# A linear-attention and expert-routing kernel: a new order of the first batch, four scaled-q buffers, loads and DMA transposes in strict turns, and the second expert's weight sums moved up into block 7

## The chip, the cores and the metric

The kernel runs on one core of a Trainium2 chip. The metric is device time in microseconds (us) of a whole execution, compared by medians and by ratios of the same rounds. The engines are called PE (TensorE), DVE (VectorE), ACT (ScalarE), POOL (GpSimd, which issues the loads) and SP (SyncE, which issues the DMA transposes).

## The reference, cut to what matters

```python
def _attn_ref(q, k, v):                      # (8, 8, 576, 64) each
    # phi(x) = concat(relu(x) * cos, relu(x) * sin) over the head dimension
    q_p, k_p = phi(q, cos_w, sin_w), phi(k, cos_w, sin_w)
    kv = np.einsum('bhsf,bhsd->bhfd', k_p, v)
    z = np.sum(k_p, axis=2)
    num = np.einsum('bhsf,bhfd->bhsd', q_p, kv)
    den = np.einsum('bhsf,bhf->bhs', q_p, z)[..., None] + 1e-06
    return num / den

def _moe_ref(x, w_gate, w1, w2):             # x (4608, 512), 8 experts, F = 1024
    P = np.exp(logits - logits.max())        # logits = x @ w_gate
    for _ in range(8):                       # the normalisation
        P /= P.sum(1, keepdims=True) + 1e-09
        P /= P.sum(0, keepdims=True) + 1e-09
        P *= N / E
    for e in range(E):
        out += P[:, e:e+1] * (np.maximum(x @ w1[e], 0.0) @ w2[e])
```

## The kernel before

The first stage is a pipeline of blocks. In block j, PE does the first expert's feed-forward for 512 tokens (16 "slots": eight of first-layer products, eight of w2 products). Between the slots stands the attention of the next batch, and the preparation of the one after it. For each batch there are two kinds of transfer: loads of q, k and v (six of 288 KB, issued by POOL), and, from the third batch on, four DMA transposes of the scaled q (issued by SP). PE reads the transposed q (in the views q_pT, acc_lo and acc_hi by the buffer that holds it) for the denominators of the next block. From block 7 on, the normalisation of the routing runs beside the products: DVE adds up P over the tokens of each partition (colp), and PE adds colp over the partitions (the product copied_ps<-colp). Stage 2, with the second expert, follows.

```python
qp_pool = p1.enter_context(tc.tile_pool(name="qp_pool", bufs=3))   # scaled q
...
def load(b, half, names="qkv", held_back=False):
    for name in names:
        ...
        i = nc.gpsimd.dma_start(out=..., in_=view[:, 2 * half : 2 * half + 2])
        if held_back:
            after(ve.last, i)            # wait for the last DVE instruction written so far
        landing[name, b, half] = i

def prep_q(b, hk):
    ...
    q_p = qp_pool.tile([P, C, 2, D], F16, name="q_p")
    ve.tensor_tensor(out=q_p[:], in0=q16..., in1=cs, op=ALU.mult)
    if by_dma:                           # b >= 2
        turned = nc.sync.dma_start(out=qTs[b, hk], in_=q_p[:]..., transpose=True)
        if b == 3 and hk == 0:
            after(landing["v", b, 1], turned)
...
# which work stands behind which slot of block j (b = j + 1); cut
for slot, fn, hk in (
    (4, prep_q, 0), (5, prep_q, 1), (8, prep_k, 0), (8, prep_q, 2),
    (9, prep_k, 1), (10, prep_kv, 0), (10, prep_k, 2), (12, prep_q, 3),
    (12, prep_kv, 1), (12, prep_k, 3), (13, prep_kv, 2), (14, prep_kp, 3),
    (14, prep_v, 3),
) if j == 1 else (
    (4, prep_q, 0), (5, prep_k, 0), (5, prep_q, 1), (6, prep_k, 1), ...
) if j == 2 else (
    (3, prep_k, 0), (4, prep_k, 1), (5, prep_q, 0), (6, prep_q, 1), ...
):
    at(j, slot, fn, b + 1, hk)
if j == 1:
    at(j, 15, sums, b + 1, 0)
    for name in "qkv":
        for half in range(2):
            at(j, 12, load, b + 2, half, name, True)
elif j and b + 2 < B:
    for half in range(2):
        at(j, 11 + half, load, b + 2, half, "qkv", True)
```

So with batches counted from one, block 1 holds the fourth batch's preparation and issues the fifth's loads; block 2 holds the fifth's preparation and issues the sixth's loads; block 3 holds the sixth's preparation, whose first k (a relu on ACT) stands in slot 3.

The second expert uses a seven-product scheme that needs sums of its w2. Before the change, DVE makes them when the second expert's first pair of row tiles begins:

```python
if name == "P1":
    if self.first:
        ve.tensor_tensor(out=tw2[0], in0=b22, in1=b12, op=ALU.subtract)
        ve.tensor_tensor(out=tw2[1], in0=tw2[0], in1=b11, op=ALU.subtract)
...
elif name == "P7":
    if self.first:
        ve.tensor_tensor(out=tw2[2], in0=b21, in1=tw2[0], op=ALU.subtract)
```

Of the kernel before, what the change touches and what calls it, by code (L numbers as in the profile page):

```python
# [25 lines left out]
def kernel(  # L26
# [185 lines left out]
    with ExitStack() as p1:  # L212
        ld = p1.enter_context(tc.tile_pool(name="ld", bufs=4))
        kp_pool = p1.enter_context(tc.tile_pool(name="kp_pool", bufs=4))
        qp_pool = p1.enter_context(tc.tile_pool(name="qp_pool", bufs=3))
        qT_pool = p1.enter_context(tc.tile_pool(name="qT_pool", bufs=1))
        kv_pool = p1.enter_context(tc.tile_pool(name="kv_pool", bufs=2))
        rb_pool = p1.enter_context(tc.tile_pool(name="rb_pool", bufs=4))
# [7 lines left out]
        landing = {}  # L226
        sources = {"q": q, "k": k, "v": v}

        def load(b, half, names="qkv", held_back=False):
            for name in names:  # L230
                x = ld.tile([P, 2, C, D], F16, name=f"{name}_ld")
                view = sources[name][b].rearrange("(hk hh) (p c) d -> (hh p) hk (c d)", hh=2, c=C)
                i = nc.gpsimd.dma_start(  # L233
                    out=x[:].rearrange("p hk c d -> p hk (c d)"),
                    in_=view[:, 2 * half : 2 * half + 2],
                )
                if held_back:

                    after(ve.last, i)
                landing[name, b, half] = i  # L240
                for i in range(2):
                    loaded[name, b, 2 * half + i] = x[:, i]
# [5 lines left out]
        load(0, 0, "q")  # L248
        gidx = cs_pool.tile([P, C], FP32, name="gidx")
# [4 lines left out]

        ones_sq = cs_pool.tile([P, P], F16, name="ones_sq")
# [6 lines left out]
        load(0, 1, "q")  # L262
        for name in "kv":
            load(0, 0, name)
            load(0, 1, name)
# [22 lines left out]
        for _ in range(74):  # L288
            keep_busy(1)
# [17 lines left out]
        for hh in range(2):  # L307
            ve.tensor_copy(
                out=cs_half[hh * HP : (hh + 1) * HP, :, :, hh],
                in_=cs[hh * HP : (hh + 1) * HP, :, :, 0],  # L310
            )
# [8 lines left out]
        C3 = C // 3  # L320

# [6 lines left out]
        with nc.allow_low_precision("sums of zeros and ones"):  # L328
# [11 lines left out]
        ones_col = const.tile([P, 1], FP32, name="ones_col")  # L340
        ve.memset(ones_col[:], 1.0)
        ones_all = const.tile([P, P], FP32, name="ones_all")
        ve.memset(ones_all[:], 1.0)
        eps_row = cs_pool.tile([1, 32], FP32, name="eps_row")
        ve.memset(eps_row[:], 1e-6 / XS)
# [8 lines left out]
        lent = acc_lo[:, G_LO - 4 : G_LO, :].rearrange("p g d -> p (g d)").bitcast(F16)  # L354
        VA = C * (D + 2)
        v_augs = [
            lent[:, i * VA : (i + 1) * VA].rearrange("p (c d) -> p c d", d=D + 2)
            for i in range(4)
        ]
# [7 lines left out]
        for t in v_augs:  # L367
            ve.memset(t[:, :, D : D + 1], 1.0 / XS)

# [7 lines left out]
        def prep_q(b, hk):  # L377

            q16 = loaded.pop(("q", b, hk))
            by_dma = b >= 2  # L380
            if by_dma:
                ve.tensor_scalar(
                    out=q16, in0=q16, scalar1=0.0, scalar2=None, op0=ALU.max
                )
            q_p = qp_pool.tile([P, C, 2, D], F16, name="q_p")
            ve.tensor_tensor(
                out=q_p[:], in0=q16.unsqueeze(2).to_broadcast([P, C, 2, D]),
                in1=cs, op=ALU.mult,
            )
            if by_dma:  # L390
                qTs[b, hk] = q_pTs[(b * HK + hk) % len(q_pTs)]
                turned = nc.sync.dma_start(
                    out=qTs[b, hk], in_=q_p[:].rearrange("p c a d -> p (c a d)"),
                    transpose=True,
                )
                if b == 3 and hk == 0:

                    after(landing["v", b, 1], turned)
            else:
                qps[b, hk] = q_p  # L400
# [76 lines left out]
        def sums_begun(b, half):  # L477
# [7 lines left out]
            kv_ps = [ps_s.tile([P, 512], FP32, name="small_ps") for hh in range(2)]  # L485
# [157 lines left out]
        for hk in range(HK):  # L643
            if hk == 3:
                prep_k(0, 0)
                prep_k(0, 1)
                z_ps = key_sums(0)
                prep_q(0, hk)
                key_sums_made(0, z_ps)
            else:  # L650
                prep_q(0, hk)
            for i in range(3):
                turn(0, hk, i, True)
                keep_busy(3)
        prep_kp(0, 0)
        prep_kp(0, 1)
        denominators(0, range(0, 4))
        keep_busy(8)
        for hk in (2, 3):
            prep_k(0, hk)  # L660
        z_ps = key_sums(1)
        prep_kp(0, 2)
        key_sums_made(1, z_ps)
        prep_kp(0, 3)
        keep_busy(5)
        denominators(0, range(4, 8))
        for half in range(2):
            sums_made(0, half, sums_begun(0, half))
            keep_busy((0, 18)[half])
# [6 lines left out]
        ]  # L676
        for hk in range(HK):
            attend(0, hk)
            for kt in ((), (0,), (1,), (2, 3))[hk]:
                for ft, h_ps in enumerate(first_ps):  # L680
                    te.matmul(
                        out=h_ps[:],
                        lhsT=w0[0][:, kt, ft * P : (ft + 1) * P],
                        rhs=xT[:, kt, 0:TCH],
                        start=(kt == 0),
                        stop=(kt == KT - 1),
                    )
                    if kt == KT - 1:
                        se.activation(out=hT[:, ft, 0:TCH], in_=h_ps[:], func=AF.Relu)
            for i in ((), (0,), (1, 2), ())[hk]:  # L690
                prep_k(1, i, i < 2)
            for i in ((), (0,), (1,), (2, 3))[hk]:
                if i == 3:
                    prep_k(1, i, False)
                prep_kp(1, i)
# [3 lines left out]
        for j in range(B):  # L699
            b = j + 1  # L700
            if j == 0:
# [4 lines left out]
                for hk in range(HK):  # L706
                    for i in range(3):
                        at(0, (5, 6, 6, 7)[hk], turn, 1, hk, i, i != 1)
                    if hk == 0:
                        at(0, 5, prep_q, 1, 3)  # L710
                    if hk == 2:
                        at(0, 6, prep_v, 1, 0, se.copy)
                        at(0, 6, prep_v, 1, 2, ve.tensor_copy)
                    if hk == 3:
                        at(0, 7, prep_v, 1, 1, se.copy)
                        at(0, 7, prep_v, 1, 3, ve.tensor_copy)
# [6 lines left out]
            elif b < B:  # L723
# [14 lines left out]
                elif j == 2:  # L738
                    at(j, 0, sums, b, 1)
                else:  # L740
                    at(j, 0, prep_kv, b, 2)
                    at(j, 1, prep_kv, b, 3)
                    at(j, 2, sums, b, 0)
                    at(j, 2, sums, b, 1)
                at(j, 6 if j == 1 else 3 if j == 2 else 4, denominators, b)
# [18 lines left out]
            elif b + 1 < B:  # L764
                for slot, fn, hk in (
                    (4, prep_q, 0), (5, prep_q, 1), (8, prep_k, 0), (8, prep_q, 2),
                    (9, prep_k, 1), (10, prep_kv, 0), (10, prep_k, 2), (12, prep_q, 3),
                    (12, prep_kv, 1), (12, prep_k, 3), (13, prep_kv, 2), (14, prep_kp, 3),
                    (14, prep_v, 3),
                ) if j == 1 else (  # L770
                    (4, prep_q, 0), (5, prep_k, 0), (5, prep_q, 1), (6, prep_k, 1),
                    (8, prep_q, 2), (8, prep_k, 2), (10, prep_q, 3), (10, prep_k, 3),
# [7 lines left out]
                if j == 1:  # L780
                    at(j, 15, sums, b + 1, 0)
            if j == 1:
                for name in "qkv":
                    for half in range(2):
                        at(j, 12, load, b + 2, half, name, True)
            elif j and b + 2 < B:
                for half in range(2):
                    at(j, 11 + half, load, b + 2, half, "qkv", True)
# [164 lines left out]
    class Pair:  # L953
# [45 lines left out]
        def step(self, name):  # L999
# [3 lines left out]
            if name == "P1":  # L1003
                if self.first:

                    tw2[0:2] = [t_pool.tile([P, FH, DH], F16, name=f"V{k_}")[:] for k_ in (2, 3)]
                    ve.tensor_tensor(out=tw2[0], in0=b22, in1=b12, op=ALU.subtract)
                    ve.tensor_tensor(out=tw2[1], in0=tw2[0], in1=b11, op=ALU.subtract)
# [4 lines left out]
            elif name == "P7":  # L1013

                if self.first:
                    tw2[2:3] = [t_pool.tile([P, FH, DH], F16, name="V4")[:]]
                    ve.tensor_tensor(out=tw2[2], in0=b21, in1=tw2[0], op=ALU.subtract)
# [36 lines left out]
    tw2 = [None] * 3  # L1054
    both = (nc.sync, nc.scalar)
# [92 lines left out]
    for j in range(B - 1, NJ):  # L1148
# [5 lines left out]
        for slot in range(NS):  # L1154
# [6 lines left out]
            if j == B - 1 and slot == 0:  # L1161
                gates(B - 1, Z[:])
            balanced({1: 3, 4: 5, 8: 5, 13: 5, 17: 5, 22: 5}.get((j - B + 1) * NS + slot, 0))
# [24 lines left out]
    def start_fill():  # L1188

        nonlocal k_fill  # L1190
        for _ in range(1 + (k_fill % 14 == 1)):
# [18 lines left out]
    for e in range(1, E):  # L1210
# [3 lines left out]
        for n in range(NU):  # L1214
# [28 lines left out]
            if e == 1 and n == 0:  # L1243
# [4 lines left out]
                w2_first(w)  # L1248
# [45 lines left out]
```

## Time and profile before

| | before |
|---|---|
| median | 975.19 us of 3 runs (974.3 to 975.83) |
| profiled span | 972.1 us, mean granted clock 0.999 |
| PE busy | 959.4 us (99%) |
| DVE / ACT / POOL busy | 807.4 / 565.0 / 60.7 us |

PE is nearly always busy, so only what makes PE wait, or what removes a wait of PE, can show in the time. The prediction below shows the lines.

### The profile page before, as it was taken

To read this page: it belongs to the slowest core of one execution; us is meant where nothing else is said; L and a number is where in the kernel's file an instruction comes from. 1 tells how busy PE (TensorE), PEld (TensorE's weight loads), DVE (VectorE), ACT (ScalarE), POOL (GpSimd) and SP (SyncE) were. 2 spreads that over 40 slices of the span, in tenths; PEclk is the share of its full clock that TensorE was granted. 3 is DMA by queue.
4 is the path that set the end of the run, shared out by engine and by line. 5 is a ranking of instruction groups with operands and counts; after the bars stand their busy time and mean duration, and the time that the engine had idled before them with its cause. 6 is when DMAs were issued, how large, how long until landed. Compare 5 with 4: busy or idle time off the path is not lost.

```text
span 972.1 us, 20258 instructions
## 1 busy us (share of the span) xinstructions
PE 959.4 (99%) x7855; PEld 674.6 (69%) x7855; DVE 807.4 (83%) x1831; ACT 565.0 (58%) x1264; POOL 60.7 (6%) x82
## 2 busy tenths in 40 slices
PE   9999999999999999999999999999999999999997
PEld 6545555567777777777777777777777777777775
DVE  7767776789898887987888987987888987987887
ACT  5767665577776555555555555555555555555551
POOL 6231210010000000000000000000000000000001
PEclk9999999999999999999999999999999999999999
DMA  9999988231004301332004301322004401115435
GB/s 162 188 154 173 156 137 184 44 69 50 26 26 93 69 25 50 68 62 57 25 26 93 69 25 51 68 54 65 26 25 86 75 25 42 33 28 124 123 90 127
DMA packets 81200, 74.72 MB, mean 77 GB/s; under 512 B 33360, under 2 KB 73040, under 8 KB 81104
## 3 DMA queue, kind: packets, MB, share of 16 engines
q0 software_dynamic: 27232, 30.94, 20.4%
q1 hardware_dynamic: 53632, 42.24, 17.8%
q8 instruction: 61, 1.00, 0.4%
q14 instruction: 35, 0.29, 0.1%
q10 hardware_dynamic: 240, 0.26, 0.1%
HBM read 84.30 MB, written 12.98 MB: 100 GB/s over the span
## 4 chain that ended last, share of the span: by engine, by line
PE 91%; DMA 4%; issue 2%; DVE 1%; POOL 1%; ACT 0%; POOLq 0%; DVEq 0%; SPq 0%; ACTq 0%
PE rows_ps L109 34%; PE h_ps L109 28%; PE p_ps L109 11%; PE copied_ps L109 11%; PE y_ps L109 4%; PE small_ps L109 3%; DMA k_ld<-in_k_dram 1%; DMA w1e<-in_moe_w_dram 1%; DMA w2e<-in_moe_w_dram 1%; DVE acc_hi L975 0%; POOL q_ld L233 0%; POOL hs_last L990 0%; DMA out_dram<-acc_lo 0%; DVE H L905 0%; DVE S L203 0%
## 5 line engine op out<-in xcount | busy, mean ns | idle before, releaser
L975 DVE SCALAR_TENSOR_TENSOR acc_lo<-rows_ps,P_tok,acc_lo 128x512 f32<-128x512 f32 (+1 forms) x322 | 203.8, 642 | 74.9 <-PE rows_ps L109 74.8
L109 PEld LDWEIGHTS <-H 128*128 128x128 f16 x2080 | 203.1, 98 | 82.3 <-issue 1.4
L911 ACT CAST u<-h_ps 128x384 f16<-128x384 f32 x288 | 137.5, 478 | 129.7 <-PE h_ps L109 129.7
L109 PEld LDWEIGHTS <-w1e 128*128 128x128 f16 x1632 | 157.7, 98 | 67.2 <-issue 5.3
L905 DVE CUSTOM_DVE_ANT_0 H<-p_ps,u 128x384 f16<-128x384 f32 x329 | 181.7, 552 | 7.2 <-PE p_ps L109 7.1
L109 PEld LDWEIGHTS <-hs 128*128 128x128 f16 x1500 | 146.6, 98 | 56.2
L109 PE MATMUL p_ps<-xT,T 128*128 128x384 f16 x672 | 164.2, 326 | 1.0 <-DVE H L905 0.9
L109 PE MATMUL h_ps<-S,w1e 128*128 128x384 f16 x672 | 164.2, 326 | 0.8 <-ACT u L911 0.6
L109 PE MATMUL rows_ps<-V,H 128*128 128x256 f16 x1000 | 150.0, 273 | 0.7 <-DVE acc_hi L975 0.7
L109 PE MATMUL rows_ps<-w2e,hs 128*128 128x256 f16 x1000 | 150.0, 273 | 0.0
L109 PE MATMUL h_ps<-xT,w1e 128*128 128x384 f16 (+1 forms) x616 | 148.8, 351 | 0.1
L943 ACT ACTIVATE H<-h_ps 128x384 f16<-128x384 f32 x144 | 70.6, 490 | 94.5 <-PE h_ps L109 94.5
L109 PEld LDWEIGHTS <-T 128*128 128x128 f16 x1008 | 98.4, 98 | 31.9 <-issue 4.9
L109 PE MATMUL rows_ps<-w2e,H 128*128 128x256 f16 (+1 forms) x568 | 94.4, 285 | 0.0
L924 ACT COPY copied_ps<-h_ps 128x384 f32<-128x384 f32 x144 | 67.5, 469 | 36.0 <-PE h_ps L109 35.2
L934 ACT ACTIVATE H<-copied_ps 128x384 f16<-128x384 f32 x144 | 70.8, 492 | 20.4 <-PE copied_ps L109 20.4
L109 PE MATMUL h_ps<-S,T 128*128 128x384 f16 x336 | 81.8, 325 | 0.6 <-ACT copied_ps L109 0.5
L109 PE MATMUL copied_ps<-xT,w1e 128*128 128x384 f16 x336 | 82.1, 326 | 0.0
L109 PE MATMUL copied_ps<-w2e,H 128*128 128x256 f16 x504 | 75.6, 273 | 0.0
L109 PE MATMUL rows_ps<-V,hs 128*128 128x256 f16 x500 | 75.0, 273 | 0.0
L975 DVE SCALAR_TENSOR_TENSOR acc_lo<-copied_ps,P_tok,acc_lo 128x256 f32<-128x256 f32 x126 | 60.3, 479 | 0.4
L975 DVE SCALAR_TENSOR_TENSOR acc_hi<-rows_ps,P_tok,acc_hi 128x512 f32<-128x512 f32 (+1 forms) x56 | 41.4, 739 | 20.6 <-PE rows_ps L109 19.7
(146 smaller groups left out, 947.7 us busy)
## 6 DMA issues: line engine op xcount, KB each, us to landing
S<-x_saved SPq DMA_DIRECT2D x114, 192.0 KB, 2.4
out_dram<-acc_lo SPq DMA_DIRECT2D x62, 128.0 KB, 2.4
w1e<-in_moe_w_dram POOLq DMA_DIRECT2D x7, 1024.0 KB, 8.8
w2e<-in_moe_w_dram POOLq DMA_DIRECT2D x7, 1024.0 KB, 9.6
q_ld<-in_q_dram POOLq DMA_DIRECT2D x16, 288.0 KB, 6.5
k_ld<-in_k_dram POOLq DMA_DIRECT2D x16, 288.0 KB, 7.8
v_ld<-in_v_dram POOLq DMA_DIRECT2D x16, 288.0 KB, 9.6
x_saved<-S SPq DMA_DIRECT2D x12, 192.0 KB, 1.8
```

The costliest lines, as they stand in the source:

```text
L109: i = getattr(self.engine, name)(*args, **kwargs)
L905: latest = ve._custom_dve(TENSOR_ADD_SAT, out=out, in0=ps[:, 0:TU], in1=t[:], s0=FP32_MAX, s1=0.0)
L911: se.copy(out=t[:], in_=ps[:, 0:TU])
L924: se.copy(out=Y[:, 0:TU], in_=X[:, 0:TU])
L934: se.activation(out=h11, in_=Y[:, 0:TU], func=AF.Relu)
L943: se.activation(out=h12, in_=X[:, 0:TU], func=AF.Relu)
L975: ve.scalar_tensor_tensor(out=a, in0=rows, scalar=P_tok[:, g, self.e : self.e + 1], in1=a, op0=ALU.mult, op1=ALU.add,)
```

## The change

The intent is to get the first expert products going earlier, to take small waits out of the second and third blocks, to keep loads and transposes from running into one another, and to move the w2 sums out of a stretch in which DVE is full. The diff, cut to its core:

```diff
-        qp_pool = ...(name="qp_pool", bufs=3)
+        qp_pool = ...(name="qp_pool", bufs=4)
-        rb_pool = ...(name="rb_pool", bufs=4)
+        rb_pool = ...(name="rb_pool", bufs=3)
+        turnings = {}
...
-                if held_back:
+                if behind is not None:
+                    after(turnings[behind], i)       # a load waits for a landed transpose
+                elif held_back:
                     after(ve.last, i)
...
-                if b == 3 and hk == 0:
+                if b in (3, 4):                      # a transpose waits for the batch's last v
                     after(landing["v", b, 1], turned)
+                turnings[b, hk] = turned
...     # the first batch: loads, scalings, sums and first products in a new order
-        for _ in range(74):
-            keep_busy(1)                             # 128 columns each
+        for _ in range(110):
+            te.matmul(...)                           # 64 columns each
...     # the slots of the fourth and the fifth batch
-                    (4, prep_q, 0), (5, prep_q, 1), (8, prep_k, 0), (8, prep_q, 2),
-                    (9, prep_k, 1), (10, prep_kv, 0), (10, prep_k, 2), (12, prep_q, 3),
-                    (12, prep_kv, 1), (12, prep_k, 3), (13, prep_kv, 2), (14, prep_kp, 3),
-                    (14, prep_v, 3),
+                    (4, prep_q, 0), (5, prep_q, 1), (9, prep_k, 0), (8, prep_q, 2),
+                    (10, prep_k, 1), (12, prep_q, 3), (12, prep_k, 2), (13, prep_k, 3),
+                    (13, prep_kv, 0), (14, prep_kv, 1),
                 ) if j == 1 else (
-                    (4, prep_q, 0), (5, prep_k, 0), (5, prep_q, 1), (6, prep_k, 1),
-                    (8, prep_q, 2), (8, prep_k, 2), (10, prep_q, 3), (10, prep_k, 3),
+                    (5, prep_q, 0), (6, prep_q, 1), (8, prep_k, 0), (8, prep_q, 2),
+                    (9, prep_k, 1), (10, prep_q, 3), (10, prep_k, 2), (11, prep_k, 3),
...
-                        at(j, 12, load, b + 2, half, name, True)
+                        at(j, 12, load, b + 2, half, name, True, (b + 1, HK - 1))
...
-                    at(j, 11 + half, load, b + 2, half, "qkv", True)
+                    at(j, 11 + half, load, b + 2, half, "qkv", True,
+                       (b + 1, HK - 1) if j == 2 else None)
...     # the second expert's w2 sums, in block 7
             if j == B - 1 and slot == 0:
                 gates(B - 1, Z[:])
+                w2_first(w_next)
+                w2_sums(w_next[1], 0)
+            if j == B - 1 and slot == 2:
+                w2_sums(w_next[1], 1)
```

## The prediction

> **What bounds the kernel now.** I read the page's busy line first, then busy time by stretches, the timelines of the engines at the places that the change touches, the waits, and the landing times of the DMAs.
>
> ```profile
> PE 959.4 (99%) x7855; PEld 674.6 (69%) x7855; DVE 807.4 (83%) x1831; ACT 565.0 (58%) x1264; POOL 60.7 (6%) x82
> ```
>
> TensorE (PE) is busy in all but 12.7 of 972.1 us, so moving work of other engines pays only where PE waits, and a new wait of PE costs its full length. The 12.7 us are the start (1.1), the end, and a few holes. Behind "busy" hides one more thing: filler products on a tile of ones. The first 74 take 5.7 us, and from 7 to 20 us another 4.4 us of PE is filler (summed from the timeline).
>
> The timelines, in order of time, one engine a row:
>
> ```profile
> 1.14 5.72 PE L109 MATMUL y_ps<-ones_sq 128*128 128x128 f16 x74 [1.14 <-DVE ones_sq L109]
> ...
> 6.83 0.77 DVE L109 TENSOR_TENSOR q_p<-q_ld,acc_hi 128x1152 f16<-128x1152 f16 x1
> ...
> 10.50 0.53 DVE L109 TENSOR_SCALAR k_ld<-k_ld 128x576 f16<-128x576 f16 x2 [1.57 <-DMA k_ld<-in_k_dram]
> ...
> 15.50 1.35 DVE L109 RECIPROCAL den<-y_ps 96x192 f32<-96x192 f32 x1
> ...
> 33.78 1.04 PE L109 MATMUL y_ps<-w2e,hT 128*128 128x512 f16 x4
> ...
> 57.89 0.68 ACT L109 ACTIVATE k_ld<-k_ld 128x576 f16<-128x576 f16 x1 [2.25 <-DMA k_ld<-in_k_dram]
> ...
> 59.48 0.46 PE L109 MATMUL small_ps<-hl,acc_hi 96*128 96x192 f16 x3 [1.11 <-ACT rb L109]
> ...
> 84.10 0.72 POOL L233 DMA_DIRECT2D q_ld<-in_q_dram  x1 [13.47 <-DVE acc_lo L109]
> ...
> 91.16 0.68 ACT L109 ACTIVATE k_ld<-k_ld 128x576 f16<-128x576 f16 x1
> ...
> 93.58 1.89 PE L109 MATMUL h_ps<-xT,w1e 128*128 128x512 f16 x8
> ...
> 163.39 0.45 DVE L109 TENSOR_REDUCE rs<-P_tok 128x36 f32<-128x288 f32 x1 [2.20 <-ACT P_tok L109]
> ...
> 166.34 0.28 PE L109 MATMUL copied_ps<-colp,ones_all 128*128 128x8 f32 x2
> ...
> 205.62 0.48 PE L109 MATMUL p_ps<-xT,T 128*128 128x384 f16 x2 [0.85 <-DVE H L905]
> ```
>
> The reader is to see: the first chain (q scaled at 6.83, k at 10.50 when it lands, reciprocal at 15.50) that decides when real products begin; a PE hole of 1.11 us at 59.48 because ACT sat on a k that had not landed; k of the sixth batch used at 91.16 without a wait, close behind its landing at 90.27; the normalisation that begins at 163.39 and feeds PE at 166.34; a hole at 205.62 behind DVE.
>
> By stretches (PE first), the last place:
>
> ```profile
> 200.00:210.00 10.00, 9.01 (x62) 5.86 (x61) 9.93 (x22) 6.69 (x15) 2.59 (x3) 1.00 0.85 157
> ```
>
> DVE is full (9.93) and PE idle for 1.0 us. The landing of w2 of the second expert, from the DMA view of its issue:
>
> ```profile
> w2e<-in_moe_w_dram POOLq DMA_DIRECT2D x1, 1024.0 KB, 17.4
> ```
>
> It is issued at 147.90, so it lands at 165.3.
>
> **What the skill says.** "TensorE: Matmul & The Clock Gate", Part 1: products of the first ~3.4 us run at half clock, and an idle window of the same length throttles again. The 74 products average 5.72/74 = 77 ns against 54 later, so it agrees; the filler must warm, and holes of 1 to 2 us should not cool. The same page's table calls the ACT and DVE queues strict FIFO; 57.89 to 59.48 shows it (a late k holds copies that were ready). "DMA: Bandwidth & Descriptors", "Issuing engines are not separate DMA queues": loads and transposes share 16 engines. Here a transpose issued at 53.6 among loads took 10.2 us to land, others 3.2 to 3.3. Same page, "Anatomy of one DMA", gives about 2.0 us plus bytes/436e9, an estimate of 2.7 us for 288 KB; the trace has 4.7 us for the first load of a group and 1.45 us for each next. I use the trace.
>
> **Part by part.** Sums are of trace durations; "before clock" means the old trace's time.
>
> *First batch.* Three copies and memsets move out of the way, so DVE reaches the first q at about 5.9 instead of 6.83; q lands at 5.95, so 5.97. Four scalings of 0.70 and the halved cosine copy (0.5) end at 9.3. k still lands at 10.47 (the load queue is full from 3 to 41 us, so order alone doesn't hasten it). From there: relu 0.5, k sums on PE to 11.7, DVE to 12.0, relu 0.5, scaled k 0.7, second k sums to 13.3, DVE 13.6, scaled k 14.3, then reciprocal 14.3 against 15.50: 1.2 us earlier. The numerators and first expert products follow with fewer holes, about 1.4 us ahead at the end of the first four column blocks (23.6 against 25.0). Then DVE binds: four scaled k (0.7), two relus (0.25), four scaled q (0.7), four evictions of turns (0.5) and now all four v copies (0.37) run from 22.6 to 32.2; the last sums need 0.65, so w2 products begin at 32.9 against 33.78. **-0.9 us.** w2 pieces land at 30.5 to 34.3, so they just hold.
>
> *Fourth batch.* k goes from slot 8 to 9, behind the copies that PE needs. Its landing, 57.87 before, comes about 1.5 us earlier, as no transpose runs among those loads. The hole of 1.11 and crumbs go: **-1.2 us.**
>
> *Strict turns.* The chain is loads(4th), transposes(4th), loads(5th), transposes(5th), loads(6th). Loads(4th) are issued at 51.03-0.9 = 50.1; five land by 50.1+4.75+4x1.45 = 60.7, say 60.9. Transposes: issued 1.4 apart, landing 3.3 after issue: last at 60.9+4.2+3.3 = 68.4. Loads(5th): six, 68.5+4.75+5x1.45 = 80.5. Transposes(5th): 88.0. Loads(6th): issued 88.1 instead of 84.10; q 92.9, k 94.3 (before 90.27). The slots of the fifth batch were moved back to fit; those of the sixth were not: ACT takes its k in slot 3, on the new clock at 91.16-2.1 = 89.1. ACT blocks until 94.3, PE has two banks and stops at its slot 6, due at 93.58-2.1 = 91.5, until 94.3+0.57+0.55 = 95.4. **+3.9 us**, and k's second half at 98.7 another +0.2.
>
> *w2 sums in block 7.* DVE gets the first difference and two sums after slot 0 of block 7. They read w2, which lands at 165.3, and DVE is in order. So 0.65+0.6+0.6 follow 165.3 and the normalisation starts at 167.15, not 163.39; its first column sums (1.15 to start, 0.67 long and 0.2 margin) are ready at 169.2, and PE, due at 166.34, waits 2.9, then 0.3 at the second. **+3.2 us.** The hole at 200 to 210 goes: idle 1.0 and looser spacing, **-1.2 us.**
>
> *Four q buffers, three reciprocal buffers:* DVE waits once, 1.2 us at 82.0, for a q buffer, off PE's path. **0.**
>
> Sum: -0.9-1.2+3.9+0.2+3.2-1.2 = **+4.0**, that is 979.2 us.
>
> **Rivals.** (a) *The turns are the gain.* Loads and transposes alone run faster than mixed, so k of the sixth batch may come in time. For: 10.2 against 3.3 us. Against: adding up even the fast durations gives 94.3. It would make 979.2-4.1 = 975. (b) *w2 lands earlier or the normalisation has slack.* For: the load shares engines with stores of sums. Against: nothing in the change moves its issue. It would make 979.2-3.2 = 976; with (a), 972. (c) *The opening gains more*, if DVE isn't the binder up to 32 us: up to 2 us more, but w2's last piece at 34.3 caps it. (d) The stop of 3.9 us cools PE (an idle window of about 3.4 us): 1 to 2 us more, 981.
>
> **Range and chances.** Both added waits come from adding landings, not from a view of the new kernel, and such slots were surely placed by someone who looked; I give each about 0.65. 979.2 less about a third of 7.3 is 976.8; I say **977.0 us**. Both waits absent and a better opening is 971, everything and a cooled clock 982: range **971 to 982**. 2% is 19.5 us; nothing here reaches that: faster 0.01, same 0.98, slower 0.01.
>
> **What would show it.** Reciprocal near 14.3; first w2 products near 32.9; no PE hole near 58; ACT idle some 5 us before a k_ld relu near 94 and PE idle some 4 us just behind; DVE idle in block 7 until w2 lands, then PE idle about 3 us ahead of the first product of colp; no hole near 205. If those two PE holes are missing, the time is 971 to 973 and my steps on landings are wrong. If the opening is wrong, DVE's work from 22 to 32 us will show idle time.

## The result, and the profile after

| | before | after |
|---|---|---|
| median, same chip | 975.51 us of 4 runs (974.3 to 979.88) | 986.47 us of 4 runs (985.04 to 987.24) |
| profiled span, mean granted clock | 972.1 us, 0.999 | 985.5 us, 0.994 |

The ratio is 1.0102, 95% interval 1.0069 to 1.0136: slower, by less than 2%. A ratio here is the mean time of one kernel's runs over the mean of the other's of the same rounds, so it is not quite the ratio of the medians. The prediction of 977.0 us, and its range of 971 to 982, missed.

The page of after has PE 2.5 us busier and the span 13.4 us longer:

```profile
PE 961.9 (98%) x7886; PEld 674.6 (68%) x7886; DVE 809.4 (82%) x1834; ACT 564.2 (57%) x1261; POOL 60.4 (6%) x82
```

To see where the time went, I took the start of the same PE instruction in both traces (us from the start of the span; the "predicted" column adds up the prediction's own steps):

```
first w2 product of block     before     after    difference   predicted
0                              33.78     32.25      -1.53        -0.9
1                              54.84     53.24      -1.60        -0.9
2                              76.47     73.78      -2.69        -2.1
3                              95.55    105.47      +9.92        +1.8
4                             114.48    125.39     +10.91        +2.0
6                             152.43    163.26     +10.83        +2.0
first product of colp         166.34    180.11     +13.77        +4.9
first product of stage 2      184.69    198.80     +14.11        +5.2
29th such product             247.79    260.50     +12.71        +4.0
last product                  967.80    980.67     +12.87        +4.0
```

Down to block 2 the rows move about as predicted (the opening gains 0.6 us more than said); then one step fails: from block 2 to block 3 the kernel loses 12.6 us instead of 3.9, and another 1.0 (predicted 0.2) up to block 4. The waits of PE in the stretch from 15 to 215 us of after (who waited, on what: us in total, times, longest) name it:

```profile
PE h_ps L109 <- ACT hT L109: 7.1, 1, 7.1
PE copied_ps L109 <- DVE colp L109: 2.8, 1, 2.8
PE small_ps L109 <- DMA q_pT<-q_p: 1.8, 1, 1.8
PE small_ps L109 <- DVE xT L109: 1.3, 1, 1.3
PE small_ps L109 <- DMA acc_hi<-q_p: 0.5, 1, 0.5
```

The timelines of after at the places the prediction named (start us, us, engine, what, then in brackets the idle time before it and what ended that):

```profile
13.82 1.35 DVE L109 RECIPROCAL den<-y_ps 96x192 f32<-96x192 f32 x1
...
32.25 1.04 PE L109 MATMUL y_ps<-w2e,hT 128*128 128x512 f16 x4
...
92.76 0.35 PE L109 MATMUL small_ps<-q_pT,zsel 128*32 128x192 f16 x6 [1.78 <-DMA q_pT<-q_p]
...
93.28 0.72 POOL L234 DMA_DIRECT2D q_ld<-in_q_dram  x1 [18.24 <-DMA q_pT<-q_p]
...
100.40 0.68 ACT L109 ACTIVATE k_ld<-k_ld 128x576 f16<-128x576 f16 x1 [10.25 <-DMA k_ld<-in_k_dram]
...
101.62 3.57 PE L109 MATMUL h_ps<-xT,w1e 128*128 128x512 f16 x8 [7.06 <-ACT hT L109]
...
175.94 0.69 DVE L109 TENSOR_TENSOR w2e<-w2e 128x1024 f16<-128x1024 f16 x1 [3.92 <-DMA w2e<-in_moe_w_dram]
...
178.01 0.45 DVE L109 TENSOR_REDUCE rs<-P_tok 128x36 f32<-128x288 f32 x1
...
180.11 0.39 PE L109 MATMUL copied_ps<-colp,ones_all 128*128 128x8 f32 x2 [2.78 <-DVE colp L109]
```

The reader is to see the predicted chain in the predicted order, only later: the sixth batch's loads go out at 93.28, when the last transpose of the fifth has landed; ACT sits 10.25 us on the first k, which lands at 100.38; PE stands 7.06 us behind ACT. The stop also cools PE's clock: the eight products at 101.62 take 3.57 us, where the same group took 1.89 in before (93.58). By stretches (after the engines' busy times come the granted clock of PE, the DMA share and GB/s):

```profile
96.00:98.00 2.00, 0.00 (x0) 0.00 (x0) 0.51 (x2) 0.00 (x0) 1.59 (x3) 0.83 1.19 192
98.00:100.00 2.00, 0.00 (x0) 0.00 (x0) 1.54 (x3) 0.00 (x0) 0.00 (x0) 0.50 1.02 127
...
106.00:108.00 2.00, 2.00 (x9) 0.94 (x8) 0.00 (x0) 1.27 (x4) 0.00 (x0) 0.61 1.30 136
```

The clock records put half clock from 97.31 to 107.55 us.

The chain that the prediction added up, against the trace of after (landing times):

```
step                                 predicted    after    added lateness
loads of the fourth batch, last v       60.9      60.72        -0.2
transposes of the fourth, last          68.4      70.20        +2.0
loads of the fifth, last v              80.5      83.54        +1.2
transposes of the fifth, last           88.0      92.72        +1.7
loads of the sixth, first k             94.3     100.38        +1.4
PE goes on in block 3                   95.4     101.62        +0.1
```

The step that failed is this sum of landings: four of its links were each 1.2 to 2.0 us too short, so k came at 100.38 and not at 94.3. The last transpose of each group took 5.0 and 4.8 us instead of 3.3; POOL issued 0.54 us after the awaited landing instead of 0.1; six loads took 12.8 us instead of 12.0; k came 7.1 us after its group was issued instead of 6.2.

That explains the size of the hole. It does not yet explain why one would take turns at all, or what happens without them, so my first theory ("take the turns away and the 10 us come back") went to the chip.

### The profile page after: what moved, and what is told of

Same layout as the page of the kernel before. It is cut to its first block, busy times and chain, and to the rows that moved or that the text cites. A ratio compares the mean times of both kernels' runs of the same rounds, so it can differ in the third digit from the quotient of the medians.

```text
span 985.5 us, 20311 instructions
## 1 busy us (share of the span) xinstructions
PE 961.9 (98%) x7886; PEld 674.6 (68%) x7886; DVE 809.4 (82%) x1834; ACT 564.2 (57%) x1261; POOL 60.4 (6%) x82
## 3 DMA queue, kind: packets, MB, share of 16 engines
q1 hardware_dynamic: 53632, 42.24, 17.4%
## 4 chain that ended last, share of the span: by engine, by line
PE 91%; DMA 5%; DVE 2%; ACT 1%; issue 1%; POOL 1%; POOLq 0%; DVEq 0%; ACTq 0%; SPq 0%
PE rows_ps L109 34%; PE h_ps L109 27%; PE copied_ps L109 11%; PE p_ps L109 11%; PE y_ps L109 4%; PE small_ps L109 3%; DMA w2e<-in_moe_w_dram 2%; DMA q_ld<-in_q_dram 1%; DMA k_ld<-in_k_dram 1%; DMA acc_hi<-q_p 1%; DMA q_pT<-q_p 0%; ACT hT L109 0%; DVE acc_hi L994 0%; POOL hs_last L1009 0%; DMA out_dram<-acc_lo 0%
## 5 line engine op out<-in xcount | busy, mean ns | idle before, releaser
L109 PEld LDWEIGHTS <-T 128*128 128x128 f16 x1008 | 98.4, 98 | 30.3 <-issue 3.2
L953 ACT ACTIVATE H<-copied_ps 128x384 f16<-128x384 f32 x144 | 70.8, 492 | 20.4 <-PE copied_ps L109 20.4
```

What stands on the lines that cost most here:

```text
L109: i = getattr(self.engine, name)(*args, **kwargs)
L953: se.activation(out=h11, in_=Y[:, 0:TU], func=AF.Relu)
```

## The experiments

Fourteen kernels ran, all correct, in four calls; each call has its own runs of before (medians 975.0, 975.9, 975.1 and 975.9 us). Ratios are to those. "Loads of the fifth batch" are written loads(5), and so on.

```
run                    what                                              median   ratio   95% interval
e1_load6_free          after, only loads(6) out of the turns             991.51   1.0166  1.0142 to 1.0190
e2_no_turns            after, no turns                                   984.96   1.0096  1.0077 to 1.0116
e3_old_w2              after, w2 sums in their old place                 982.06   1.0068  1.0051 to 1.0086
e8_warm                after, filler products in the hole                984.44   1.0086  1.0063 to 1.0110
f2_opening             only opening and buffers of the change            974.48   0.9991  0.9964 to 1.0018
f4_opening_turns       f2 plus turns                                     979.01   1.0030  1.0011 to 1.0049
e11_late5              e2, loads(5) later                                984.34   1.0085  1.0066 to 1.0104
f3_opening_spread      f2, w2 sums spread over block 7                   974.00   0.9976  0.9956 to 0.9995
e13_late5_q3           e11, three q buffers                              979.82   1.0034  1.0016 to 1.0052
e14_late56             e11, loads(6) later too                           976.97   1.0007  0.9990 to 1.0024
e4_slots6              after, sixth batch's slots later                  984.23   1.0090  1.0070 to 1.0110
f5_spread_l5           f3, loads(5) one slot later                       972.14   0.9967  0.9949 to 0.9984
e16_T_free             after, transposes don't wait for v                981.43   1.0062  1.0049 to 1.0075
e15_late56_spread      e14, w2 sums spread over block 7                  971.58   0.9957  0.9944 to 0.9971
```

### e1_load6_free and e2_no_turns: the turns taken away

```diff
 e1:  -   (b + 1, HK - 1) if j == 2 else None,
      +   None,
 e2, on top of e1:
      -   at(j, 12, load, b + 2, half, name, True, (b + 1, HK - 1))
      +   at(j, 12, load, b + 2, half, name, True)
      -   if b in (3, 4):
      +   if b == 3 and hk == 0:
```

> The changed kernel, only the sixth batch's loads no longer wait for the fifth batch's transposes. My theory (the chain of turns is late and ACT blocks on the sixth k): loads of the sixth batch go out near 83 instead of 93.3, its first k lands near 90 instead of 100.4, the PE hole of 7.1 us and the half clock behind it (about 3 us) go, so about 976 us, 10 below the changed kernel. If the block is not due to that wait (a rival: the transposes or the slots alone are the cost), it stays within 2 us of 986.

> The changed kernel with loads and transposes free as before (only the fourth batch's first transpose waits for its loads), the moved slots kept. My theory: all of the 13.6 us that the trace shows between the second and the third block's products and before goes, about 972 us. Rival, turns pay by running loads and transposes alone: it loses something against the kernel without only the sixth batch's wait, so over 976.

Both missed. e1 took 991.51 us (989.46 to 994.28), slower than after; e2 took 984.96 (984.58 to 985.13), hardly faster. The longest PE wait of each, from the same view as above:

```profile
PE small_ps L109 <- DMA q_pT<-q_p: 10.5, 4, 5.4
```

```profile
PE small_ps L109 <- DMA acc_lo<-q_p: 8.7, 1, 8.7
```

The hole behind ACT's k is gone, and PE now waits for transposes. In e1 loads(6) go out at 82.06, 1.5 us ahead of the fifth batch's first transpose (83.52), which takes 12.0 us. In e2 the wait is in block 2, for the fourth batch's. The DMA view of 60 to 75 us says why. First before, then e2 (issues: out<-in, count, median us from issue to landing):

```profile
acc_lo<-q_p SPq DMA_TRANSPOSE x1, 3.4
acc_hi<-q_p SPq DMA_TRANSPOSE x1, 5.6
```

```profile
acc_lo<-q_p SPq DMA_TRANSPOSE x1, 14.4
acc_hi<-q_p SPq DMA_TRANSPOSE x1, 11.9
```

And POOL's rows for loads(5), first before, then e2:

```profile
66.33 1.43 POOL L233 DMA_DIRECT2D q_ld<-in_q_dram  x2 [11.71 <-DVE acc_lo L109]
```

```profile
62.62 1.44 POOL L234 DMA_DIRECT2D q_ld<-in_q_dram  x2 [8.98 <-DVE q_p L109]
```

The fourth batch's last two transposes are issued at 64.6 and 66.1 in before, 64.4 and 67.8 in e2. In before the loads come just behind them. In e2 they come 1.7 us in front of the first of the two. The new slots took 2.2 us of k and v work away from DVE ahead of the instruction that the loads wait for, which is most of the 3.7 us by which the loads moved forward (66.33 to 62.62). The transposes did not move with them. Among loads the two take 14.4 and 11.9 us instead of 3.4 and 5.6.

The Trainium skill, "DMA: Bandwidth & Descriptors", section "Queues, rings and completion order", says that each DMA engine goes round its queues packet by packet. The trace does not contradict that. In this stretch of after the four transposes have these packets (packets, MB, share):

```profile
q1 hardware_dynamic: 4736, 1.18, 41.8%
```

That is 4736/4/16 = 74 packets of some 250 bytes per engine and transpose, while a load's packets carry 1.1 KB (392 packets, 0.43 MB in the same view). Following loads of 288 KB land 1.45 us apart with some 260 such packets, 16 per engine, so 0.09 us each. A transpose that lets one load packet pass for each of its own waits 74 x 0.09 = 6.7 us more than the 3.3 alone, about 10 us: an estimate from that page's rule and these numbers, which takes what the profile counts as a packet for what the page calls one. The traces show 8.6 to 15.8 us (f3, and a transpose of e11). The rule itself no run shows, so why a transpose among loads is slow stays open; that it is slow is measured.

So the theory changed: loads that get in front of transposes are what costs; the turns are a cure for what the new slots brought about, and a cure with a price of its own.

### e3_old_w2: the w2 sums where they were

```diff
-                w2_first(w_next)
-                w2_sums(w_next[1], 0)
-            if j == B - 1 and slot == 2:
-                w2_sums(w_next[1], 1)
+    (both back in the second expert's first pair, as in before)
```

> The changed kernel with the second expert's w2 sums back in the first pair. My theory: the PE hole of 2.8 us in front of the first colp product goes and the hole of about 1.4 us near the first pair comes back, so 984.7, 1.8 below the changed kernel. Rival (the sums in block 7 are a gain or neutral): 986.5 or more.

Measured 982.06 us (980.73 to 984.23) where 984.7 was expected, and 1.0068 against 1.0102 for after. (The move of the sums carries another rule for handing out filler tiles in these blocks with it; e3, f2 and f4 put that back too, so it is not told apart.) The stop at colp is gone from the waits and the one near 205 is back. From the first w2 product of block 6 to the 29th product of stage 2, the trace has 95.09 us against 97.24 in after: the move costs 2.1 us, as expected (1.8). The rest of the gain is a shorter hole in block 3 in that run, 5.5 instead of 7.1 us; up to there the two kernels are the same, so landing times differ that much from one execution to the next.

### e8_warm: filler products in the hole

```diff
+                if j == 3 and slot == 5:
+                    for _ in range(30):
+                        te.matmul(out=warm_ps[:, 0:TCH], lhsT=ones_sq[:], rhs=..., ...)
```

> The changed kernel with 30 filler products of 512 columns (6.5 us at full clock) in front of the block-3 hole, which PE would otherwise spend waiting. If the half clock from 97.3 to 107.6 us costs 3 us by itself, PE stays at full clock and the time falls to about 983.5. If the clock costs nothing, it stays at 986.5; if the filler is longer than the hole, it rises.

Measured 984.44 us (982.93 to 985.48), ratio 1.0086 against 1.0102, mean clock 0.998 against 0.994. The median is near the 983.5 expected, but the interval of the ratio overlaps that of after, so the size rests on the trace. From the first product behind the hole to block 4's first w2 product, e8 takes 21.79 us (101.07 to 122.86) and after 23.77 (101.62 to 125.39): the cooled clock costs about 2 us here, on top of the stop. (In e8 k landed at 99.01, 1.4 us earlier than in after, and the fillers ran up to 0.8 us longer than it needed.)

### f2_opening, f4_opening_turns and f3_opening_spread: parts alone

f2 is the changed kernel with the slots, loads, transposes and w2 sums of before. f4 adds the turns. f3 is f2 with the w2 sums behind the normalisation's first column sums instead of in front:

```diff
 f3:
-            if j == B - 1 and slot == 0:   # w2_first, w2_sums 0; w2_sums 1 at slot 2
+            if j == B - 1 and slot == 5:
+                w2_first(w_next)
+            if j == B - 1 and slot in (10, 14):
+                w2_sums(w_next[1], (slot - 10) // 4)     # one sum each
+            if j == B and slot == 2:
+                w2_sums(w_next[1], 2)
```

> The opening, four q buffers and three reciprocal buffers of the changed kernel; slots, loads, transposes and w2 sums as before. If the loss lies in the new slots and turns (theory now): no hole of over 2 us in blocks 1 to 3, the 1.5 us of the opening stay, end about 973.5, 1.5 us under the kernel before. Rival, the buffers or the earlier opening themselves make loads and transposes collide: a hole of 5 us or more for q_pT or acc_lo, end 978 or later.

> The same as the run with the opening alone, plus the strict turns, in the slots of before. If the turns alone make the sixth batch late (each batch's loads plus transposes measured 22 us against a block of 19): first k of the sixth batch lands near 100, ACT's wait for it some 9 us, PE's hole 6 us or more in block 3, end about 982. Rival, the turns hurt only with the new slots: hole under 3 us, end under 977.

> Candidate: the opening alone, slots and loads as before, and the w2 sums of the second expert spread over block 7 from slot 5 on, behind the column sums instead of in front. Expected: no PE hole at the first colp product, no hole near ST2 either, end 1 to 1.5 us under the run with the opening alone, about 972.3. Rival, the sums delay the normalisation here too: hole of 2 us or more, end at 974 or later.

f2: 974.48 us (972.4 to 981.27). The median is near what the theory says (973.5), but the profiled run is the 981.27 one, and it has the rival's hole:

```profile
PE small_ps L109 <- DMA acc_hi<-q_p: 6.8, 1, 6.8
```

So the rival is right too, in at least this execution: the earlier opening alone shifts DVE's and SP's order by tenths of a microsecond, and that decides. Six traces, in order of that margin, tell it. All are about the fourth batch's last transpose and the first load of the fifth batch:

```
trace       transpose issued   load issued   load behind by   transpose took   PE's wait for it
f2               64.86            64.46           -0.40            12.3             6.8
f3               64.82            64.83           +0.01             8.6             2.7
before           66.08            66.33           +0.25             5.6             none listed
f5               65.36            66.41           +1.05             4.9             none listed
e14              64.78            67.09           +2.31             3.2             none listed
after            65.17            70.74           +5.57             5.0             0.5
```

The other ten traces fit: e2's margin of -5.15 us goes with 11.9 us, margins of 0.96 (e11) to 5.40 (e8) with 3.2 to 5.0 us.

Before stands at the edge: a quarter of a microsecond separates it from a hole. (Its own runs reach from 974 to 980 us; that the slow ones are this race is likely and not shown.) The 5.0 of after, where nothing of the fifth batch runs, shows a second, smaller spread that is not of this race; a fetch of instructions lies in that stretch on a DMA queue, but no run tells whether it is the cause.

f4: 979.01 us, 1.0030. The turns cost 0.4% on the old slots. First k is taken at 97.82 and ACT waits 4.06 us for it, less than expected, since the chain ran faster in this execution:

```profile
97.82 0.68 ACT L109 ACTIVATE k_ld<-k_ld 128x576 f16<-128x576 f16 x1 [4.06 <-DMA k_ld<-in_k_dram]
```

The turns on the old slots cost 4.5 us by the medians and 3.8 by the ratios (f2's mean holds the 981.27), near the +4.1 that I had predicted for them. That is luck and does not confirm the sum: here the first k lands at 97.80 and not at 94.3, PE reaches the slot that needs it near 96.2 and not at 91.5, and the two errors nearly cancel. f4 against e3 differs in the slots alone: 1.0030 against 1.0068. They were run at other times.

f3: 974.00 us, 0.9976, at the rival's number and not at 972.3: its trace has a 2.7 us hole, from the transpose race of the table and not from the sums. The w2 sums work when they stand behind the column sums: from the first w2 product of block 6 to colp the trace has 13.91 us, as in before, and from the first to the 29th product of stage 2 61.70 instead of 62.83 in f2.

### e11_late5, e13_late5_q3 and e14_late56: not turns, only a later place

```diff
 e11, on top of e2:
-                        at(j, 12, load, b + 2, half, name, True)
+                        at(2, 1, load, b + 2, half, name, True)     # loads(5)
 e13, on top of e11:
-        qp_pool = ...(name="qp_pool", bufs=4)
+        qp_pool = ...(name="qp_pool", bufs=3)
 e14, on top of e11:
-                        j, 11 + half, load, ...                      # loads(6)
+                        *((3, 0) if j == 2 else (j, 11 + half)), load, ...
```

> New slots, no turns (as the run without turns, 985.0), but the fifth batch's loads are issued some 4 us later, behind the DVE work of block 2's first slot, so that they start when the last transpose of the fourth batch has been issued. If the 8.7 us hole there came from those loads overtaking the transposes: hole gone, transposes land by 71, end about 976.3. Rival, the hole comes from the new slots as such (transposes late because q is scaled late): transposes still land after 75 and the end stays above 982.

> As the run with the late fifth loads (984.3), but three q buffers instead of four. Theory now: with three, DVE must wait for a landed transpose before it scales the fourth q, and the sixth batch's loads, which stand behind that in DVE's order, can't overtake the transposes; with four this brake is gone. Then: loads of the sixth batch issued at 83 to 86 instead of 81.1, the fifth batch's transposes landed by 90 instead of 98.4, the 7.9 us hole in block 3 gone or under 2 us, end about 977. Rival, the buffers don't matter: hole stays, end 983 to 985.

> As the run with the late fifth loads, but four q buffers and the sixth batch's loads held to the DVE work of block 3's first slot. Theory: they are issued near 86, when the last transpose of the fifth batch has been issued, transposes land by 89, no hole for q_pT; k of the sixth batch lands near 93, up to 2 us late for its slot; end about 977 to 978. Rival, the hole in block 3 is due to something else: end above 982.

e11 missed in the time (984.34 us) and hit in its place: the hole in block 2 is gone (from the first w2 product of block 1 to that of block 2 the trace has 20.4 us against 31.7 in e2), and the same hole stands one block later. The waits, and the fifth batch's transposes in the DMA view of 75 to 95 us:

```profile
PE small_ps L109 <- DMA q_pT<-q_p: 8.3, 2, 7.9
```

```profile
q_pT<-q_p SPq DMA_TRANSPOSE x4, 11.4
```

Loads(6) go out at 81.07 there, in front of the third and fourth transpose. In before they go out at 84.10, behind the fourth. What held them back is a line of DVE's timeline that the prediction had valued at nothing (before):

```profile
82.01 0.76 DVE L109 TENSOR_TENSOR q_p<-q_ld,acc_hi 128x1152 f16<-128x1152 f16 x1 [1.23 <-DMA q_pT<-q_p]
```

With three buffers, DVE can't scale the fourth q of a batch before a transpose has landed, and the loads stand behind that scaling in DVE's order. The short wait is a brake. e13 puts the third buffer back: DVE waits at that place (e13),

```profile
83.86 0.76 DVE L109 TENSOR_TENSOR q_p<-q_ld,acc_hi 128x1152 f16<-128x1152 f16 x1 [5.34 <-DMA q_pT<-q_p]
```

loads(6) go out at 85.96, the transposes land by 87.9 instead of 98.4, and the hole of 7.9 us is gone. The median is 979.82 us, 4.5 us less than e11 (in another call), not the 7 expected: the 5.34 us of DVE delay the rows of xT that it makes next, and PE waits 2.6 us for those instead.

e14 keeps four buffers and only writes loads(6) later. POOL, then (e14):

```profile
67.09 1.43 POOL L234 DMA_DIRECT2D q_ld<-in_q_dram  x2 [13.69 <-DVE acc_lo L109]
...
84.21 0.72 POOL L234 DMA_DIRECT2D q_ld<-in_q_dram  x1 [12.81 <-DVE acc_lo L109]
```

Both follow the issue of the last transpose (64.78 and 82.67), not its landing. No group of PE waits in the blocks sums to over 0.7 us, and the time is 976.97 us (974.83 to 977.54): the new slots, four buffers and no turns, 1.0007 against 1.0096 for e2. This settles the cause: what e2 and e11 lose is the order of loads and transposes, and it takes only the issue order to mend it.

### e4_slots6 and e16_T_free: which part of the turns costs

```diff
 e4:  -                ) if j == 2 else (
      +                ) if j in (2, 3) else (        # the sixth batch takes the fifth's slots
 e16: -                if b in (3, 4):
      +                if b == 3 and hk == 0:
```

> The changed kernel with its turns, but the sixth batch's preparation in the later slots that the fifth has (first k in slot 8 instead of 3). If the 7.1 us hole is there because k lands late for its slot: ACT takes k some 5 us later, the hole shrinks to 0 to 2 us, no half clock, end about 978. Rival, what is late then is the next link, transposes of the sixth batch for block 4: a hole of 4 us or more in block 4, end 982 or later.

> The changed kernel, but its transposes don't wait for the last v to land (as in the kernel before, except the fourth batch's first); the loads keep waiting for the transposes. If that half of the rule costs most: transposes of the fifth batch are issued from 75 on while loads still run, land by 88 instead of 92.7, first k of the sixth batch lands near 95 instead of 100.4, the hole in block 3 shrinks from 7.1 to about 2 us, end about 979. Rival, the other half (loads wait for the landing of transposes) costs it: k at 99 or later, end 984 or later.

e4: 984.23 us, 1.0090 against 1.0102. The hole behind ACT's k is gone, so k was late for its slot, as said. The time came back only in part in the next link, and not where the rival had it (a hole of 4 us or more in block 4, behind transposes). From block 2's to block 3's first w2 product e4 takes 22.6 us against 31.7 in after, 9.1 less. Its trace then has a hole behind DVE, in block 3 again:

```profile
103.42 0.64 PE L109 MATMUL small_ps<-hl,acc_hi 96*128 96x192 f16 x3 [2.68 <-DVE xT L109]
```

and from block 3's to block 4's first w2 product it takes 23.2 us instead of 19.9 in after (18.9 in before), with two stretches at half clock in blocks 3 and 4. Another 1.3 us are lost from colp to stage 2, where the clock falls too (20.03 us, 18.69 in after). I had not expected this much; a chain that is late as a whole was not mended at one place.

e16: 981.43 us, 1.0062. The fifth batch's transposes are issued from 73.8 on and land by 87.9, loads(6) go out at 88.43, and ACT takes k at 94.42:

```profile
94.42 0.68 ACT L109 ACTIVATE k_ld<-k_ld 128x576 f16<-128x576 f16 x1 [5.65 <-DMA k_ld<-in_k_dram]
```

PE stands 4.4 us, not the 2 expected. So transposes that wait for v cost 4 to 5 us of after (1.0102 to 1.0062; medians 986.47 to 981.43); loads that wait for landed transposes cost about as much again (e16 to e14: 1.0062 to 1.0007).

### f5_spread_l5 and e15_late56_spread: the better versions

f5 is f3 with loads(5) at slot 13 instead of 12; e15 is e14 with the spread w2 sums of f3.

> Candidate: the earlier candidate (974.0, in whose profile the last transpose of the fourth batch was issued within 0.01 us of the first load of the fifth, landed at 73.5 and held PE up 2.7 us), with those loads one slot later, behind the DVE work that follows. Theory: transpose lands at 71 or before, no hole in block 2, end about 971.5, runs less spread. Rival, later loads make the fifth batch late: a hole in block 2 or 3 for k or q, end 974 or later.

> The run with both loads held to later slots (977.0) plus the w2 sums spread over block 7. If the new slots as such cost nothing: the 2.6 us at the first colp product and the 1 us near 205 go and the end is 972 to 973.5, equal to the version with the old slots (972.1). Rival, the new slots cost in themselves: end at 975 or later.

f5: 972.14 us (971.44 to 975.04), 0.9967; no PE wait for a transpose. e15: 971.58 us (970.91 to 972.65), 0.9957: the fastest, 0.43% under before, with a spread of 1.7 us. Both beat both kernels. PE goes through the first column sums without idle time in e15:

```profile
165.94 0.28 PE L109 MATMUL copied_ps<-colp,ones_all 128*128 128x8 f32 x2
```

So no cost of the new slots by themselves is seen, and whether they gain anything over the old ones is not shown: 0.9957 and 0.9967, and their intervals overlap. They were run at other times.

From e14 to e15 the w2 sums' place is worth 5.4 us in the medians (4.9 by the ratios); the two profiled runs show 3.1 of it: 2.8 at colp and 0.3 behind it. A part of the rest is the clock. In after (a stop of 2.78 us at colp) it stayed at 1.00. In e11 (3.0 us) it did not:

```profile
180.00:182.00 2.00, 2.00 (x6) 0.68 (x5) 1.86 (x5) 0.88 (x2) 0.00 (x0) 0.50 0.00 0
```

There, from colp to the first product of stage 2 takes 20.13 us, against 18.69 in after and 18.34 without a stop; e13, with the same 3.0 us, has 21.59. In five of e14's six timed runs the mean clock was 0.997 or 0.998 (0.999 in the profiled one), in all of e15's 0.999 to 1.000, so this fall is common in e14.

The length of a stop does not decide whether the clock falls. e8's stop of 2.08 us was followed by half clock, e16's of 3.06 us was not:

```profile
176.89 0.39 PE L109 MATMUL copied_ps<-colp,ones_all 128*128 128x8 f32 x2 [2.08 <-DVE colp L109]
177.16:180.57 3.41, 3.41 (x11) 1.17 (x11) 3.24 (x8) 0.60 (x1) 0.00 (x0) 0.50 0.00 0
```

```profile
174.30 0.39 PE L109 MATMUL copied_ps<-colp,ones_all 128*128 128x8 f32 x2 [3.06 <-DVE colp L109]
173.01:176.42 3.41, 2.12 (x11) 1.12 (x12) 3.24 (x9) 0.60 (x1) 0.00 (x0) 1.00 0.01 4
```

In all 16 traces the changes of the clock lie multiples of 3.41 us apart. Cut into stretches on that grid, PE's busy share tells them apart: all 29 stretches at full clock with PE busy 42% or less were followed by half clock, none with 49% or more was, and 44 to 48% went either way. e8's stop lay in one stretch (173.75 to 177.16, PE busy 1.32 of 3.41 us, 39%); e16's was split over two (48% and 62%). So where a stop of 2 to 3 us falls on that grid matters, and not its length alone.

## Why the prediction was wrong, point by point

- **First batch, predicted -0.9:** measured -1.5. Right in kind: the reciprocal starts at 13.82 (14.3 said), the w2 products at 32.25 (32.9 said). The 0.5 us at the reciprocal are those by which k landed earlier than the prediction held (9.97, not 10.47). One reading was off without harm: of the 74 fillers the first 26 start 107 ns apart and the rest 57 to 59, not 54.
- **Fourth batch, predicted -1.2:** measured -1.1 from block 1 to block 2, and the hole behind ACT near 58 is gone. Right.
- **Strict turns, predicted +3.9 and +0.2: the step that failed.** Measured +12.6 and +1.0. The mechanism is as told (a late k, ACT in order, PE behind it); the sum of landings was too short. It put k at 94.3 and PE's going on at 95.4; k landed at 100.38, and PE went on at 101.62 after a hole of 7.06 us. That is 9.5 us more than the 4.1 predicted: 6.2 from the chain of landings, where I used fast durations of before for every link (3.3 us for each transpose, 1.45 for each next load, 0.1 from landing to issue); about 2.0 from the half clock (e8), which I had as rival (d) at 1 to 2 us and not in the sum; some 1.3 are not accounted for. I then shaded the sum down because "such slots were surely placed by someone who looked". Nothing in the profile said so.
- **w2 sums in block 7, predicted +3.2 and -1.2:** measured +2.9, +0.3 and -1.4. Right; e3 and e15 confirm it. w2 took 17.2 us to land (17.4 in before), so rival (b) did not come in. Missing was that a stop here can cool the clock as well: it did in e1, e4, e8, e11 and e13, not in after. The prediction's "holes of 1 to 2 us should not cool" is not safe either: one of 2.08 us did in e8.
- **Four q buffers, predicted 0:** wrong as an argument, though the turns hide it in after. The 1.23 us that DVE waited for a buffer kept the sixth batch's loads behind the fifth's transposes. It was off PE's path and still set when transfers started; e11 and e13 show it.
- **Rival (a), "the turns are the gain":** half right. Mixed transposes are slow, four times slower in places. But before mostly kept a batch's loads behind the transposes of the batch before, which I could have seen from its issue times (66.08 for the last transpose, 66.33 for the first load); the one that I quoted, issued at 53.6 and landed 10.2 us later, was an exception.

The sum of the measured steps (-1.5 - 1.1 + 13.6 + 3.2 - 1.4) is +12.8 us; the profiled spans differ by 13.4 and the medians by 11.0.

## What to carry to other kernels

When a chain of transfers is laid end to end, size each link by its slowest duration under like conditions in the trace, not its fastest, and compare the sum with the period that it must fit: here some 22 us from one batch's loads to the next against a block of 19. Where transposes and bulk loads run at the same time, look at the order in which they are issued: here it was enough to issue the loads behind the transposes, and waiting for landings, in both directions, spent the latency of each. Before giving an engine another buffer, ask what its wait was holding back.

## What the Trainium skill lacked or had wrong

- "DMA: Bandwidth & Descriptors" says that transfers of different issuers interleave; it gives no size for a DMA transpose among loads. Here it took 8.6 to 15.8 us from issue to landing, against 3.2 to 3.4 alone, and an issue order that differed by 0.65 us (-0.40 to +0.25) moved it from 12.3 to 5.6 us.
- The same page, "Anatomy of one DMA", would give an estimate of 2.7 us for a load of 288 KB. The first load of a group took 4.2 to 4.7 us from issue to landing (after: 93.28 to 97.43).
- No page was found to give a figure for the time from a landing, as the profile shows it, to an issue that waits for it: POOL issued 0.54 and 0.56 us after it (after: 70.20 to 70.74 and 92.72 to 93.28).
- No page says that the last of four transposes may take longer than the others with no load about: 5.0 and 4.8 us in after, 3.2 in e14.
- "TensorE: Matmul & The Clock Gate", Part 1, puts the fall of PE's clock after an idle window of about 3.4 us. The 7.06 us hole agrees (half clock from 97.31, 2.8 us into the hole, to 107.55). But the window need not be idle: here every stretch of 3.41 us with PE busy 42% or less was enough (e8: 39%, with a stop of only 2.08 us), none with 49% or more was, and a stop of 3.06 us split over two stretches did not cool (e16).
